# Attention on one Trainium2 core: the running sums of exponentials go from two engines to one

## The chip, the core and the metric

The kernel runs on one core of a Trainium2 chip. The core has five engines that work at the same time, each on its own queue of instructions in the order in which they were issued: TensorE (PE in the profile, with its weight loads shown apart as PEld), VectorE (DVE), ScalarE (ACT), GpSimd (POOL) and SyncE (SP), which here only issues DMA transfers. An instruction that has to wait for another engine holds up all that stands behind it on its own engine. The metric is the device time of one execution in microseconds. Lower is better.

## The reference

Three layers follow one another: attention with pooled queries, a gated feed-forward layer with RMS normalisation, and a mixture of experts with the best two of eight. The change touches the first alone, of which this is the core (batch 2, 8 heads, 1152 keys, head size 64, 576 pooled queries):

```python
q_pool = q.reshape(B, H, S // factor, factor, D).mean(axis=3)     # factor 2
scores = scale * np.matmul(q_pool, k.transpose(0, 1, 3, 2))
scores = scores - np.max(scores, axis=-1, keepdims=True)
attn = np.exp(scores)
attn = attn / (np.sum(attn, axis=-1, keepdims=True) + 1e-09)
return np.matmul(attn, v).astype(np.float32)
```

What matters below is `np.sum(attn, axis=-1)`: for each query, the sum of 1152 exponentials.

## The kernel before

Attention is worked through in 8 pairs of heads (p = 0 to 7; `NPB`), four to each batch entry. A pair has 18 steps: two halves of the queries (g, 288 each) times nine blocks of 128 keys (c). In each step `st_exp` (L198) makes the scores of 128 keys by 288 queries for both heads in PSUM (tile `st`, three buffers), and ScalarE turns them into exponentials in SBUF (tile `et`, 128 x 2 x 288, nine buffers). Keys lie on the partitions. `avmm` (L230) multiplies the exponentials by V, some steps later and in bursts (`S_AV`).

The sum over keys is made in two parts. First the nine `et` tiles of a half are added element by element into one tile of 128 partitions; then `sums` (L243) lets TensorE add up the partitions with a matmul by ones, and `sums2` (L257) brings the result to the queries' layout as `rs`. The first part is `esum` (L213), called once a step for the step before. The table `S_EP` says which engine takes a block: VectorE adds blocks 0, 2, 3, 4, 6 and 7 into `es` (five instructions, L222 for the first, L224 for the others), GpSimd adds blocks 1, 5 and 8 into `accp` (two instructions). `emerge` (L226) then adds `accp` to `es` on VectorE (L228), at the half-step that `S_EM` names. So a half costs VectorE six instructions and GpSimd two, and there are 16 halves.

The maximum that is subtracted is found from scores of their own: `s1` (L186) makes the scores of 128 queries against all 1152 keys in a PSUM tile of three banks, of which there is one buffer, and VectorE takes the maximum of each row into a column of `Ql` (L194). The next `s1` can't begin before that reduction is over. There are nine a pair. In the main loop those of pair p that are still open and the first of pair p + 1 stand at half-steps 1, 6, 10, 13, 16, 20, 21, 26 and 28 (`S_S1A`, `S_S1B`; half-steps count from 0 to 35, two to a step). `ql_trans` (L172) and `ql_trans2` (L178) transpose `Ql` on TensorE, at half-steps 29, 33 and 15; all transposes share one PSUM buffer (tag `T`), which must be read out before the next one is made.

All order is written out by hand: the code issues the instructions of every engine in the order of the loop at L439 to L513, and the tables name the half-step of each piece of work (`F[i]`). Besides the above, GpSimd splits K and Q of pair p + 2 into a rounded part and a remainder (`split`, at half-steps 20 and 24: L109 and L115 for K, L122, L109 and L124 for Q); it does this in pairs 0 to 5. In pairs 4 and 5 the finished first batch entry is transposed and scaled by `rs` (`x1`: TensorE L292, VectorE L293, then ScalarE and GpSimd L299); `x1` of tokens 1 to 4 stands in pair 5 at half-steps 10, 26, 27 and 30. In pair 6 `x2b` transposes it back (TensorE L324, ScalarE L327, VectorE L328). In pair 7 the decoding of the next layer's weights begins (VectorE L407 to L412, ScalarE L405 and L415, GpSimd L416). After attention the feed-forward layer's matmuls (L551) follow on TensorE.

Of the kernel before, what the change touches and what calls it, by code (L numbers as in the profile page):

```python
# [9 lines left out]
F32 = mybir.dt.float32  # L10
# [5 lines left out]
ALU = mybir.AluOpType  # L16
# [5 lines left out]
def fused_kernel(ctx, tc, q, k, v, w_gate, w_val, w_out, rms_g,  # L22
                 r_gate, r_noise, noise, e_w1, e_w2, out, dbg=None):
    nc = tc.nc
    P = 128
    B, H, S, D = q.shape
    NP = H // 2
    KC = S // P
# [4 lines left out]
    NG = 288  # L33
# [3 lines left out]
    pe, dve, act, pool, sp = nc.tensor, nc.vector, nc.scalar, nc.gpsimd, nc.sync  # L37
# [24 lines left out]
    NPB = B * NP  # L62
# [4 lines left out]
    ab = ax.enter_context(tc.tile_pool(name="ab", bufs=1))  # L67
# [21 lines left out]
    def load_kq(p, h):  # L89
        b, hh = p // NP, 2 * (p % NP) + h  # L90
        qr = Qraw[h]
        qv = q[b, hh].rearrange("(s t) d -> s (t d)", t=2)
        raw[p, h] = fr.tile([P, KC, D], F32, name="kraw", tag=f"kraw{h}", bufs=1)
        sp.dma_start(raw[p, h], k[b, hh].rearrange("(p c) d -> p c d", c=KC))
        sp.dma_start(qr[:, 0:4, :], qv[0:QF].rearrange("(p c) x -> p c x", c=4))
        if h == 1:
            for z in range(2):
                sp.dma_start(qr[z * QR:(z + 1) * QR, 4, :], q[b, hh - 1 + z].rearrange("(s t) d -> s (t d)", t=2)[QF:])
# [94 lines left out]
                pe.matmul(t[:, j, 0:384], QB, KJ[:, ks], start=True, stop=True)  # L193
        dve.tensor_reduce(Ql[p % 2][h][:, c, D:D + 1], t[:, :, 0:384], axis=AX.XY, op=ALU.max, negate=True)  # L194

    xT, rs, es, ET, AV, accp, smS = {}, {}, {}, {}, {}, {}, {}

    def st_exp(p, g, c, hs=(0, 1), early=False):  # L198
        if hs[0] == 0:
            ET[p, g, c] = ab.tile([P, 2, NG], F32, name="et", tag="et", bufs=9)  # L200
        et = ET[p, g, c]
        cs, n0 = slice(c * P, (c + 1) * P), g * NG
        for h in hs:
            if early:
                t = tpool[0].tile([P, 512], F32, name="st", tag="T")
                tpool.append(tpool.pop(0))
            else:
                t = ps[0].tile([P, 512], F32, name="st", tag="st", bufs=3)
            pe.matmul(t[:, 0:NG], KT[p, h][:, cs], QhT[p, h][:, n0:n0 + NG], start=True, stop=False)  # L209
            pe.matmul(t[:, 0:NG], KT2[h][p % NKT[h]][:, cs], QlT[p, h][:, n0:n0 + NG], start=False, stop=True)  # L210
            act.activation(et[:, h, :], t[:, 0:NG], AF.Exp, scale=SCALE)  # L211

    def esum(p, g, c):  # L213
        if g == 0 and c == 0:
            es[p] = ab.tile([P, 2, SQ], F32, name="es", tag="es", bufs=2)
        if c == 0:
            accp[p, g] = ab.tile([P, 2, NG], F32, name="accp", tag="accp", bufs=2)
        eg, ap, e = es[p][:, :, g * NG:(g + 1) * NG], accp[p, g], ET[p, g, c]
        z = S_EP[c]
        eng, acc, cs = (dve, eg, EPL[0]) if z == 0 else (pool, ap, EPL[1])  # L220
        if c == cs[1]:
            eng.tensor_tensor(acc, ET[p, g, cs[0]], e, op=ALU.add)  # L222
        elif c > cs[1]:
            eng.tensor_tensor(acc, acc, e, op=ALU.add)  # L224

    def emerge(p, g):  # L226
        eg = es[p][:, :, g * NG:(g + 1) * NG]
        dve.tensor_tensor(eg, eg, accp[p, g], op=ALU.add)  # L228

    def avmm(p, g, c):  # L230
        b, hp = p // NP, p % NP
        if c == 0:
            AV[p, g] = ps[0].tile([P, 512], F32, name="av", tag="av", bufs=1)
        av = AV[p, g]
        for h in range(2):
            pe.matmul(av[h * D:(h + 1) * D, 0:NG], V[p][:, h, c, :], ET[p, g, c][:, h, :],  # L236
                      start=(c == 0), stop=(c == KC - 1))
        if c == KC - 1:
            if g == 0:
                xT[p] = xp.tile([P, SQ], F32, name="xT", tag="xT", bufs=6)  # L240
            act.copy(xT[p][:, g * NG:(g + 1) * NG], av[:, 0:NG])  # L241
# [176 lines left out]
    S_S1A = (1, 6, 16, 13, 20)  # L418
    S_S1B = (10, 5, 21, 26, 28)
    S_KA = (0, 5, 2, 7)  # L420
    S_KB = (8, 18, 12, 20)
    S_QA = (14, 29)
    S_QB = (15, 33)
    S_SPA = 24
    S_SPB = 20
    S_EM = (12, 33)
    S_SUM = (17, 22)
    S_LD = (4, 34, 34)
    S_AV = (1, 5, 10, 13)
    S_X = (26, 10, 26, 27, 30, 33)  # L430
    S_X2 = (6, 22, 27, 31)
    S_EP = (0, 1, 0, 0, 0, 1, 0, 0, 1)
    S_LAG = 2
    S_W = ((1, 3, 4, 5, 8), (12, 18, 19, 20, 27), (30, 31, 32))

    S_LAST = dict(s1a=(0, 9), s1b=(12,), qa=(15,), em=(16, 28), sum=(20, 35), av=(1, 5, 7, 13, 16))
    EPL = [[c for c in range(KC) if S_EP[c] == z] for z in range(2)]
    av_q, n_av = [], 0
    for p in range(NPB):  # L439
        F = [[] for _ in range(2 * NST)]  # L440

        def at(i, f, *a):
            F[i].append((f, a))

        if p + 1 < NPB:
            at(S_LD[0], load_v, p + 1)
            for i in range(2, QC):
                at(S_S1A[i], s1, p + 1, 0, i - 2)
                at(S_S1B[i], s1, p + 1, 1, i - 2)
            for i in range(4):  # L450
                if p or i >= K_EARLY:
                    at(S_KA[i], kq_trans, p + 1, 0, i)
                at(S_KB[i], kq_trans, p + 1, 1, i)
            at(max(S_KA), kt2_copy, p + 1, 0)
            at(max(S_KB), kt2_copy, p + 1, 1)
            at(S_QA[1], ql_trans, p + 1, 0)
            at(S_QB[1], ql_trans, p + 1, 1)
        sl = S_LAST if p == NPB - 1 else dict(s1a=S_S1A, s1b=S_S1B, qa=S_QA, em=S_EM, sum=S_SUM, av=S_AV)
        at(sl["s1a"][0], s1, p, 0, 3)
        at(sl["s1b"][0], s1, p, 1, 3)  # L460
        at(sl["s1a"][1], s1, p, 1, 4)
        at(sl["qa"][0], ql_trans2, p)
        if p + 2 < NPB:
            if p == 0:
                load_kq(2, 0)
                load_kq(2, 1)
            at(S_SPA, split, p + 2, 0)
            at(S_SPB, split, p + 2, 1)
        if p == 1:
            for i in range(9):  # L470
                at(4 * i, lambda i: sp.dma_start(out[i * P:(i + 1) * P], zt), i)
        if p + 3 < NPB:
            at(S_LD[1], load_kq, p + 3, 0)
            at(S_LD[2], load_kq, p + 3, 1)
        if p:
            at(sl["em"][0], emerge, p - 1, 1)
            at(sl["sum"][0], sums, p - 1)
            at(sl["sum"][1], sums2, p - 1)
        at(sl["em"][1], emerge, p, 0)
        if p == NP:  # L480
            at(S_X[0], x1, 0, 0)
        if p == NP + 1:
            for i in range(1, QC):
                at(S_X[i], x1, 0, i)
            at(S_X[5], xr, 0)
        if p == NP + 2:
            for t, s_ in enumerate(S_X2):
                at(s_, x2, 0, t)
                at(s_ + 4, x2b, 0, t)
        if p == NPB - 1:  # L490
            fr_s.close()
            wps.append(ctx.enter_context(tc.tile_pool(name="wp", bufs=1, side="right", reuse_waits="tile")))
            at(0, w_load, 0, 0)
            at(0, w_load, 0, 1)
            for i, a in enumerate(((0, 0), (0, 1), (1, 0))):
                for k_, s_ in enumerate(S_W[i]):
                    at(s_, w_dec, *a, k_)
                if i < 2:
                    at(S_W[i][3], w_load, 1, i)
        for i in range(NST):  # L500
            g, c = divmod(i, KC)
            st_exp(p, g, c, (1,) if p == 0 and i < N_EARLY else (0, 1))
            av_q.append((p, g, c))
            for f, a in F[2 * i]:
                f(*a)
            if len(av_q) > 1:
                esum(*av_q[-2])
            if i in sl["av"]:
                while n_av < len(av_q) - S_LAG:
                    avmm(*av_q[n_av])  # L510
                    n_av += 1
            for f, a in F[2 * i + 1]:
                f(*a)  # L513
    esum(*av_q[-1])
    emerge(NPB - 1, 1)
    for a in av_q[n_av:]:
        avmm(*a)
    ax.close()
# [1129 lines left out]
```

## Time and profile before

| | |
|---|---|
| median of three runs | 777.85 us (776.69 to 778.9) |
| the profiled execution | 776.33 us |
| its span | 774.6 us |
| TensorE busy | 740.6 us (96% of the span) |
| VectorE busy | 528.6 us (68%) |
| ScalarE busy | 375.1 us (48%) |
| GpSimd busy | 256.7 us (33%) |
| granted TensorE clock, mean | 0.994 of full speed |

The profile comes from one execution. The span runs from its first instruction to its last; the device time has some 1.7 us around it. Busy time is the time in which an engine has an instruction in work; for TensorE matmuls overlap, so that a busy TensorE need not be at its peak. Attention fills the stretch from about 20 to 264 us. One pair takes about 30 us, and pair p begins near the start of its reduction at half-step 1: 21.43, 49.56, 171.70, 204.10 and 236.53 us for pairs 0, 1, 5, 6 and 7.

### The profile page before, as it was taken

What the parts mean: (1) busy time and instruction counts of PE and PEld (TensorE: products, weight loads), DVE (VectorE), ACT (ScalarE), POOL (GpSimd) and SP (SyncE); (2) the same over time, 40 slices, a digit from 0 to 9 for tenths busy, and PEclk for the clock granted to TensorE, in tenths of its full rate; (3) what the DMA queues carried; (4) which work ended last, traced back from release to release, by engine and by line L of the source; (5) the groups of instructions that cost most, each with busy time, mean ns of one, the idle gap of its engine ahead of it and who ended that gap; (6) DMA issues with size and microseconds to landing.
All of it is one profiled execution on the core that took longest, in us unless ns stands there. A gap on an engine that the chain in (4) does not pass through costs nothing. (4 is left out here: it accounts for less than half of the span.)

```text
span 774.6 us, 13461 instructions
## 1 busy us (share of the span) xinstructions
PE 740.6 (96%) x5078; PEld 613.0 (79%) x5078; DVE 528.6 (68%) x804; ACT 375.1 (48%) x766; POOL 256.7 (33%) x219
## 2 busy tenths in 40 slices
PE   6999999999999999999999999999999999999993
PEld 5777777777676669988888889987998898978761
DVE  6788778878779877657568745569756676748520
ACT  5556565656667554443142325254544455537510
POOL 8456366375713321222022310020312212432221
PEclk9999999999999999999999999999999999999997
DMA  8556243333251221332033201664998769879982
GB/s 234 146 151 186 71 124 84 93 94 91 52 150 55 67 99 55 104 113 87 23 110 109 58 1 55 218 188 153 322 358 259 212 169 278 257 239 362 351 269 46
DMA packets 74010, 118.02 MB, mean 152 GB/s; under 512 B 7383, under 2 KB 37807, under 8 KB 73936
## 3 DMA queue, kind: packets, MB, share of 16 engines
q1 hardware_dynamic: 68784, 106.27, 43.6%
q0 software_dynamic: 5152, 10.80, 6.4%
q8 instruction: 42, 0.69, 0.4%
q14 instruction: 32, 0.26, 0.1%
HBM read 98.16 MB, written 9.65 MB: 139 GB/s over the span
## 5 line engine op out<-in xcount | busy, mean ns | idle before, releaser
L551 PE MATMUL gv<-XN,ws 128*128 128x256 f32 (+2 forms) x912 | 164.8, 330 | 1.3 <-POOL ws L416 1.3
L551 PEld LDWEIGHTS gv<-XN,ws 128*128 128x128 f32 x912 | 143.3, 188 | 15.7 <-POOL ws L416 1.9
L194 DVE TENSOR_REDUCE Ql<-s 128x1 fp32r<-128x1152 f32 x72 | 97.4, 1355 | 48.7 <-PE s L191 31.9
L211 ACT ACTIVATE et<-st 128x288 f32<-128x288 f32 x288 | 103.6, 417 | 41.5 <-PE st L210 39.2
L1101 DVE TENSOR_TENSOR wz<-raw,wz 128x1024 fp32r<-128x1024 f32 x80 | 96.0, 1223 | 28.9 <-ACT wz L107 28.6
L1202 PE MATMUL py<-wz,hTT 128*128 128x512 f32 x384 | 93.8, 395 | 0.0
L209 PE MATMUL st<-QH,KT 128*128 128x288 f32 x288 | 91.5, 333 | 2.3 <-ACT et L211 1.2
L416 POOL TENSOR_TENSOR ws<-wm,ws 128x1024 fp32r<-128x1024 f32 x18 | 43.6, 2423 | 145.2 <-ACT ws L415 130.2
L572 PE MATMUL po<-ws,hT 128*128 128x512 f32 x324 | 83.2, 395 | 2.2 <-DVE X L577 2.1
L107 ACT CAST wz<-raw 128x1024 fp32r<-128x1024 f32 x80 | 81.1, 1047 | 0.4 <-PE py L1202 0.4
L210 PE MATMUL st<-QlT,KT 128*128 128x288 f32 x288 | 81.1, 295 | 0.0
L1202 PEld LDWEIGHTS py<-wz,hTT 128*128 128x128 f32 x384 | 70.0, 188 | 13.6 <-DVE hTT L1070 0.2
L236 PE MATMUL av<-et,v 128*64 128x288 f32 x576 | 77.4, 412 | 0.5 <-ACT xT L241 0.5
L209 PEld LDWEIGHTS st<-QH,KT 128*128 128x128 f32 x288 | 54.0, 187 | 22.2 <-issue 12.3
L572 PEld LDWEIGHTS po<-ws,hT 128*128 128x128 f32 x324 | 58.9, 188 | 14.2 <-DVE X L577 3.2
L224 DVE TENSOR_TENSOR es<-es,et 128x576 f32<-128x576 f32 x64 | 63.4, 991 | 1.6
L1278 POOL DMA_INDIRECT out_dram<-yo,sidx x16 | 29.3, 1832 | 96.9 <-DVE yo L1277 55.9
L236 PEld LDWEIGHTS av<-et,v 128*64 128x64 f32 x576 | 38.3, 136 | 27.8 <-issue 3.9
L1175 PEld LDWEIGHTS ph<-xgT,wz 128*128 128x128 f32 x480 | 57.7, 189 | 0.4
L1175 PE MATMUL ph<-xgT,wz 128*128 128x256 f32 x480 | 57.8, 281 | 0.0
L561 ACT CAST hT<-sl 128x256 fp32r<-128x256 f32 (+2 forms) x38 | 18.9, 497 | 74.9 <-DVE sl L560 74.9
L210 PEld LDWEIGHTS st<-QlT,KT 128*128 128x128 f32 x288 | 54.3, 189 | 0.2
(280 smaller groups left out, 1097.0 us busy)
## 6 DMA issues: line engine op xcount, KB each, us to landing
raw<-in_moe_w_dram SPq DMA_DIRECT2D x112, 512.0 KB, 9.0
wraw<-in_moe_w_gate_dram SPq DMA_DIRECT2D x6, 1024.0 KB, 6.8
wraw<-in_moe_w_val_dram SPq DMA_DIRECT2D x6, 1024.0 KB, 5.0
wraw<-in_moe_w_out_dram SPq DMA_DIRECT2D x6, 1024.0 KB, 4.8
kraw<-in_k_dram SPq DMA_DIRECT2D x16, 288.0 KB, 3.7
v<-in_v_dram SPq DMA_DIRECT2D x8, 576.0 KB, 3.7
KT<-KT SPq DMA_DIRECT2D x16, 288.0 KB, 3.1
KJ<-KT SPq DMA_DIRECT2D x16, 288.0 KB, 4.6
```

The source lines that it names most:

```text
L107: act.copy(o, i)
L194: dve.tensor_reduce(Ql[p % 2][h][:, c, D:D + 1], t[:, :, 0:384], axis=AX.XY, op=ALU.max, negate=True)
L209: pe.matmul(t[:, 0:NG], KT[p, h][:, cs], QhT[p, h][:, n0:n0 + NG], start=True, stop=False)
L210: pe.matmul(t[:, 0:NG], KT2[h][p % NKT[h]][:, cs], QlT[p, h][:, n0:n0 + NG], start=False, stop=True)
L211: act.activation(et[:, h, :], t[:, 0:NG], AF.Exp, scale=SCALE)
L224: eng.tensor_tensor(acc, acc, e, op=ALU.add)
L236: pe.matmul(av[h * D:(h + 1) * D, 0:NG], V[p][:, h, c, :], ET[p, g, c][:, h, :], start=(c == 0), stop=(c == KC - 1))
L551: pe.matmul(t[:, 0:n], w[a][:, d, j * P:(j + 1) * P], XN[hf][b_][:, d, cs], start=(k_ == 0), stop=(k_ == 11))
L572: pe.matmul(pt, HT[f, hf][a][:, j, c0:c0 + P], w[b_][:, j, :], start=(k_ == 0), stop=(k_ == 5))
L1101: eng.tensor_tensor(lo, RAW[u % 2][i], hi.bitcast(F32), op=ALU.subtract)
L1175: pe.matmul(o, w[a][:, d, j * P:j * P + P], XT[u][c][:, d], start=z + d == 0, stop=z == 2 and d == 3)
L1202: pe.matmul(PL[u, "y", k], x[c][:, f0 + d, k * P:k * P + P], w[a][:, d], start=i == 4 and z + d == 0, stop=i == 7 and z == 2 and d == 1)
```

## The change

GpSimd's share of the sums goes. `esum` adds all nine blocks of a half into `es` on VectorE: one instruction for blocks 0 and 1 together, then seven more. `accp`, `emerge` and the tables `S_EP`, `EPL` and `S_EM` are gone, and nothing else is edited.

```diff
     def esum(p, g, c):
         if g == 0 and c == 0:
             es[p] = ab.tile([P, 2, SQ], F32, name="es", tag="es", bufs=2)
-        if c == 0:
-            accp[p, g] = ab.tile([P, 2, NG], F32, name="accp", tag="accp", bufs=2)
-        eg, ap, e = es[p][:, :, g * NG:(g + 1) * NG], accp[p, g], ET[p, g, c]
-        z = S_EP[c]
-        eng, acc, cs = (dve, eg, EPL[0]) if z == 0 else (pool, ap, EPL[1])
-        if c == cs[1]:
-            eng.tensor_tensor(acc, ET[p, g, cs[0]], e, op=ALU.add)
-        elif c > cs[1]:
-            eng.tensor_tensor(acc, acc, e, op=ALU.add)
-
-    def emerge(p, g):
-        eg = es[p][:, :, g * NG:(g + 1) * NG]
-        dve.tensor_tensor(eg, eg, accp[p, g], op=ALU.add)
+        eg, e = es[p][:, :, g * NG:(g + 1) * NG], ET[p, g, c]
+        if c == 1:
+            dve.tensor_tensor(eg, ET[p, g, 0], e, op=ALU.add)
+        elif c > 1:
+            dve.tensor_tensor(eg, eg, e, op=ALU.add)
...
-    S_EM = (12, 33)
...
-    S_EP = (0, 1, 0, 0, 0, 1, 0, 0, 1)
...
-    EPL = [[c for c in range(KC) if S_EP[c] == z] for z in range(2)]
...
         if p:
-            at(sl["em"][0], emerge, p - 1, 1)
             at(sl["sum"][0], sums, p - 1)
             at(sl["sum"][1], sums2, p - 1)
-        at(sl["em"][1], emerge, p, 0)
...
     esum(*av_q[-1])
-    emerge(NPB - 1, 1)
```

Eight lines fewer stand ahead of most of the code, so that L222 becomes L218, L224 becomes L220, L293 becomes L285 and so on. How the instructions now follow one another on VectorE is shown at three places.

VectorE in pair 0, from the reduction at half-step 1 to the one at half-step 13, before (`Ql<-s` is the maximum of an `s1` tile, `es<-et` the first add of a half, `es<-es,et` a further one):

```order
L194 TENSOR_REDUCE Ql_91<-s_329 128x1
L194 TENSOR_REDUCE Ql_92<-s_356 128x1
L222 TENSOR_TENSOR es<-et 128x2x288
L224 TENSOR_TENSOR es<-es,et 128x2x288
L194 TENSOR_REDUCE Ql_92<-s_383 128x1
L224 TENSOR_TENSOR es<-es,et 128x2x288
L194 TENSOR_REDUCE Ql_93<-s_409 128x1
```

and after:

```order
L194 TENSOR_REDUCE Ql_91<-s_329 128x1
L218 TENSOR_TENSOR es<-et 128x2x288
L194 TENSOR_REDUCE Ql_92<-s_356 128x1
L220 TENSOR_TENSOR es<-es,et 128x2x288 x2
L194 TENSOR_REDUCE Ql_92<-s_383 128x1
L220 TENSOR_TENSOR es<-es,et 128x2x288 x2
L194 TENSOR_REDUCE Ql_93<-s_409 128x1
```

The first add of the half, now of blocks 0 and 1, stands ahead of the reduction at half-step 6, and two adds instead of one follow each of the next two reductions.

VectorE in pair 1, from the reduction at half-step 21 over the one at 26 to the one at 28, before (`rs` is the result of `sums2`):

```order
L194 TENSOR_REDUCE Ql_92<-s_882 128x1
L266 TENSOR_SCALAR rs_812<-xt 128x2x2 x2
L268 TENSOR_SCALAR rs_812<-xt 64x2
L222 TENSOR_TENSOR es<-et 128x2x288
L194 TENSOR_REDUCE Ql_92<-s_931 128x1
L224 TENSOR_TENSOR es<-es,et 128x2x288
L194 TENSOR_REDUCE Ql_92<-s_953 128x1
```

and after:

```order
L194 TENSOR_REDUCE Ql_92<-s_879 128x1
L258 TENSOR_SCALAR rs_810<-xt 128x2x2 x2
L260 TENSOR_SCALAR rs_810<-xt 64x2
L218 TENSOR_TENSOR es<-et 128x2x288
L220 TENSOR_TENSOR es<-es,et 128x2x288
L194 TENSOR_REDUCE Ql_92<-s_929 128x1
L220 TENSOR_TENSOR es<-es,et 128x2x288
L194 TENSOR_REDUCE Ql_92<-s_951 128x1
```

Between the reductions at half-steps 21 and 26 there are now two adds, one right behind the other, where there was one. The same holds in every pair up to pair 6.

VectorE in pair 5, from the reduction at half-step 21 to the one at 28, before (`xs<-xt,rs` is the scaling in `x1`, which frees the transposes' PSUM buffer):

```order
L194 TENSOR_REDUCE Ql_92<-s_2418 128x1
L266 TENSOR_SCALAR rs_2349<-xt 128x2x2 x2
L268 TENSOR_SCALAR rs_2349<-xt 64x2
L222 TENSOR_TENSOR es<-et 128x2x288
L194 TENSOR_REDUCE Ql_92<-s_2466 128x1
L293 TENSOR_TENSOR xs_2072<-xt,rs_812 128x512
L224 TENSOR_TENSOR es<-es,et 128x2x288
L293 TENSOR_TENSOR xs_2073<-xt,rs_812 128x512
L194 TENSOR_REDUCE Ql_92<-s_2506 128x1
```

and after:

```order
L194 TENSOR_REDUCE Ql_92<-s_2407 128x1
L258 TENSOR_SCALAR rs_2339<-xt 128x2x2 x2
L260 TENSOR_SCALAR rs_2339<-xt 64x2
L218 TENSOR_TENSOR es<-et 128x2x288
L220 TENSOR_TENSOR es<-es,et 128x2x288
L194 TENSOR_REDUCE Ql_92<-s_2456 128x1
L285 TENSOR_TENSOR xs_2064<-xt,rs_810 128x512
L220 TENSOR_TENSOR es<-es,et 128x2x288
L285 TENSOR_TENSOR xs_2065<-xt,rs_810 128x512
L194 TENSOR_REDUCE Ql_92<-s_2496 128x1
```

The added instruction is again the second add ahead of the reduction at half-step 26, and with it ahead of both scalings `xs`. On GpSimd the 32 adds into `accp` are gone, and the order of the rest is as it was; TensorE, ScalarE and SyncE issue the same instructions in the same order.

## Rows read from the trace of the kernel before

**Rows 1.** The page, part 1: busy us, share of the span, instructions

```profile
PE 740.6 (96%) x5078; PEld 613.0 (79%) x5078; DVE 528.6 (68%) x804; ACT 375.1 (48%) x766; POOL 256.7 (33%) x219
```

**Rows 2.** Busy time of one stretch: stretch, length, busy us (instructions) by engine

```profile
100.00:120.00 20.00, 19.87 (x145) 15.33 (x145) 15.67 (x16) 12.01 (x34) 10.50 (x8) 1.00 0.44 119
```

**Rows 3.** Groups by line, to 300 us: xcount | busy us, mean ns

```profile
L224 DVE TENSOR_TENSOR es<-es,et 128x576 f32<-128x576 f32 x64 | 63.4, 991 | 1.6
L228 DVE TENSOR_TENSOR es<-es,accp 128x576 f32<-128x576 f32 x16 | 18.2, 1136 | 0.3 <-issue 0.3
L222 DVE TENSOR_TENSOR es<-et 128x576 f32<-128x576 f32 x16 | 13.4, 839 | 0.0
L222 POOL TENSOR_TENSOR accp<-et 128x576 f32<-128x576 f32 x16 | 27.1, 1694 | 48.7 <-ACT et L211 48.7
L224 POOL TENSOR_TENSOR accp<-accp,et 128x576 f32<-128x576 f32 x16 | 26.0, 1625 | 33.4 <-ACT et L211 28.3 <-DVE es L224 4.7
```

**Rows 4.** Waits, 20 to 270 us: total us, times, longest us

```profile
PEld s L191 <- DVE Ql L194: 2.8, 10, 0.4
```

**Rows 5.** Timeline, pair 0, VectorE, then TensorE: start, us, instruction, [idle before]

```profile
25.80 1.88 DVE L224 TENSOR_TENSOR es<-es,et 128x576 f32<-128x576 f32 x1
27.60 1.34 DVE L194 TENSOR_REDUCE Ql<-s 128x1 fp32r<-128x1152 f32 x1
...
25.08 0.79 PE L191 MATMUL s<-KT,QH 128*128 128x384 f32 x3
29.00 0.79 PE L191 MATMUL s<-KT,QH 128*128 128x384 f32 x3 [0.28 <-DVE Ql L194]
```

**Rows 6.** Timeline, pair 1, VectorE, then GpSimd, then TensorE

```profile
69.33 1.21 DVE L222 TENSOR_TENSOR es<-et 128x576 f32<-128x576 f32 x1
71.82 1.29 DVE L224 TENSOR_TENSOR es<-es,et 128x576 f32<-128x576 f32 x1
...
69.27 0.67 POOL L109 TENSOR_SCALAR khl<-kraw 128x576 fp32r<-128x576 f32 x1
70.02 1.78 POOL L115 TENSOR_TENSOR khl<-kraw,khl 128x576 fp32r<-128x576 f32 x1
71.77 0.73 POOL L122 TENSOR_TENSOR qs<-Qraw 128x256 f32<-128x256 f32 x1
...
72.68 0.69 PE L191 MATMUL s<-KT,QH 128*128 128x384 f32 x3
```

**Rows 7.** Timeline, pair 2, VectorE, then GpSimd

```profile
99.66 0.74 DVE L222 TENSOR_TENSOR es<-et 128x576 f32<-128x576 f32 x1
...
99.61 1.32 POOL L109 TENSOR_SCALAR khl<-kraw 128x576 fp32r<-128x576 f32 x1
```

**Rows 8.** Timeline, pair 4, VectorE, then GpSimd, then TensorE

```profile
160.76 0.77 DVE L222 TENSOR_TENSOR es<-et 128x576 f32<-128x576 f32 x1
...
161.01 1.78 POOL L115 TENSOR_TENSOR khl<-kraw,khl 128x576 fp32r<-128x576 f32 x1
...
164.11 0.69 PE L191 MATMUL s<-KT,QH 128*128 128x384 f32 x3
166.28 0.37 PE L136 MATMUL tt<-identr,Ql 128*128 128x128 f32 x3
```

**Rows 9.** Timeline, pair 5, VectorE, then GpSimd, then TensorE

```profile
191.56 1.21 DVE L222 TENSOR_TENSOR es<-et 128x576 f32<-128x576 f32 x1
194.10 0.68 DVE L293 TENSOR_TENSOR xs<-xt,rs 128x512 f32<-128x512 f32 x1
...
192.25 1.79 POOL L115 TENSOR_TENSOR khl<-kraw,khl 128x576 fp32r<-128x576 f32 x1
...
194.83 0.66 PE L292 MATMUL xt<-ident,xT 128*128 128x128 f32 x4
```

**Rows 10.** Timeline, TensorE, end of pair 6 and start of the next stage

```profile
233.59 0.45 PE L136 MATMUL tt<-identr,Ql 128*128 128x128 f32 x3 [0.87 <-DVE XN L328]
270.16 0.55 PE L262 MATMUL xt<-ident,smS 128*128 128x128 f32 x3 [0.61 <-ACT smS L255]
```

More of the change, by code (lines that the diff above doesn't have):

```diff
@@ L194, in s1 @@
         dve.tensor_reduce(Ql[p % 2][h][:, c, D:D + 1], t[:, :, 0:384], axis=AX.XY, op=ALU.max, negate=True)
-    xT, rs, es, ET, AV, accp, smS = {}, {}, {}, {}, {}, {}, {}
+    xT, rs, es, ET, AV, smS = {}, {}, {}, {}, {}, {}
     def st_exp(p, g, c, hs=(0, 1), early=False):
@@ L431, in fused_kernel @@
     S_X2 = (6, 22, 27, 31)
-    S_EP = (0, 1, 0, 0, 0, 1, 0, 0, 1)
     S_LAG = 2
     S_W = ((1, 3, 4, 5, 8), (12, 18, 19, 20, 27), (30, 31, 32))
-    S_LAST = dict(s1a=(0, 9), s1b=(12,), qa=(15,), em=(16, 28), sum=(20, 35), av=(1, 5, 7, 13, 16))
-    EPL = [[c for c in range(KC) if S_EP[c] == z] for z in range(2)]
+    S_LAST = dict(s1a=(0, 9), s1b=(12,), qa=(15,), sum=(20, 35), av=(1, 5, 7, 13, 16))
     av_q, n_av = [], 0
@@ L457, in fused_kernel @@
             at(S_QB[1], ql_trans, p + 1, 1)
-        sl = S_LAST if p == NPB - 1 else dict(s1a=S_S1A, s1b=S_S1B, qa=S_QA, em=S_EM, sum=S_SUM, av=S_AV)
+        sl = S_LAST if p == NPB - 1 else dict(s1a=S_S1A, s1b=S_S1B, qa=S_QA, sum=S_SUM, av=S_AV)
         at(sl["s1a"][0], s1, p, 0, 3)
```

## The prediction

> **What bounds the kernel now.** I read the page first: TensorE is busy 96% of the span, VectorE 68%, GpSimd 33% [rows 1]. Then the busy time by stretch: in the middle of attention TensorE has 19.87 of 20 us, VectorE 15.67 and GpSimd 10.50 [rows 2]. So TensorE sets the pace, VectorE has about a fifth of its time free, and an engine's load as such decides nothing. What can cost time is a place where TensorE waits for one particular VectorE instruction. There are two kinds: the next `s1` needs the reduction of the one before it (one buffer), and a transpose needs the shared `T` buffer, which in pairs 4 to 6 a VectorE instruction frees. The waits show how tight the first kind is already: ten waits of TensorE's weight loads for a reduction, 2.8 us in all, none over 0.4 [rows 4]. Little is lost there, but little is left. I then read the timelines around each of these places.
>
> **What is removed and added.** VectorE adds into `es` 96 times before: 63.4 + 18.2 + 13.4 = 95.0 us [rows 3]. An undisturbed add takes 0.74 to 0.75 us [rows 7], so 96 would take 72; the other 23 us are VectorE standing still inside an add while GpSimd works on SBUF. The 32 adds into `accp` (27.1 + 26.0 us, rows 3) are one part of that, the splits of K and Q the other. After the change there are 16 x 8 = 128 adds, 96 us if undisturbed. VectorE is thus as busy as before, and GpSimd has 53 us less. No other engine gets or loses an instruction, no DMA is moved. What counts is which collisions go and which are new.
>
> **Pair 0, collision gone.** The add at 25.80 lasts 1.88 us with GpSimd's first `accp` add beside it, so the next reduction starts at 27.60 although its scores were ready at 25.87 (25.08 + 0.79). The following `s1` waits 0.28 us for it [rows 5]. In the new order two adds precede that reduction, which end about 26.4, and the wait goes: -0.3. What is late next is the reduction after it, behind two adds as well, but they fit into the time in which TensorE makes its scores. Bounds: 0 (another wait takes over) and -0.6 (the next `s1` gains as much again).
>
> **Half-steps 21 to 28 in pairs 1 to 5.** Here GpSimd splits K and Q, and the new order puts a second add right behind the first, ahead of the reduction at half-step 26. Pair 1 [rows 6]: GpSimd's L109 begins at 69.27 and VectorE's first add at 69.33; the add takes 1.21 instead of 0.75, so it waited until GpSimd was through, and ends at 70.54. GpSimd's next instruction, L115, asks at 70.02, stands until the add is over and ends at 71.80. The new second add would ask at 70.47, later than L115. I let the one that asked first go first, since the same timeline shows it once more: L122 from 71.77 takes its undisturbed 0.73, and the add from 71.82 takes 1.29, to 73.11, 0.61 us after L122's end. So the second add ends at 71.80 + 0.61 = 72.41, the reduction starts there and lasts 1.34 to 1.36 [rows 5], and ends about 73.70. The next `s1` follows a reduction's end by 0.06 (27.60 + 1.34 = 28.94, then 29.00, rows 5): 73.76 instead of 72.68. TensorE loses 1.1 us. In front of this `s1` nothing on TensorE can be brought forward, and all that stands behind it moves with it. Pair 3 has the same rows in the trace, with a first add of 1.21 as well: another 1.1.
>
> Pair 2 differs: VectorE's add from 99.66 takes 0.74, and GpSimd's L109 from 99.61 takes 1.32 instead of 0.67 [rows 6, 7]. Here VectorE went first. The second add then waits only for the short L109, until about 100.9, ends about 101.5, and the reduction ends about 102.9, just ahead of the `s1` that needs it (as in pair 1, 3.35 us after the first add, 103.0): 0, with bounds 0 and 1.1.
>
> At this place the Trainium skill has a rule ("SBUF — State Buffer", section "SBUF: two separate sides"): VectorE and GpSimd share a pair of ports as an exclusive lock, and whichever starts first has it for its whole instruction. Pairs 1 and 3 agree (GpSimd 0.06 us earlier, VectorE's add 1.21). Pair 2 does not: GpSimd started 0.05 us earlier and yet it was the one that waited. By the rule alone pair 2 would cost 1.1 as well, and the sum would be +6.1 instead of +5.0.
>
> Pair 4 [rows 8]: the first add runs from 160.76 to 161.53 undisturbed, L115 asks at 161.01 and ends at 162.79. The second add ends at 162.79 + 0.61 = 163.40, the reduction about 164.7, and the `s1` at 164.11 comes 0.6 late. Then its own reduction: between the two stand a scaling of 0.68 and another add, with GpSimd's last split instructions beside them. 164.7 + 0.6 + 0.7 is 166.0, the reduction ends about 167.4, and the transpose at 166.28 that reads its result comes at 167.4: +1.1. Bounds: 0 (second add not held up) and 1.7 (the third add held up in full too).
>
> Pair 5 [rows 9]: first add until 192.77, L115 until 194.04, second add until 194.65, reduction until about 195.95. Behind it stands the scaling (0.68, until 196.55), and for that the transposes at 194.83 wait: 196.6, so +1.8. Bounds: 0.5 (second add not held up: 193.45, reduction 194.75, scaling 195.35) and 2.4 (the same again at the next scaling).
>
> **Pairs 6 and 7 and the way out.** There is no split any more. In pair 6 the transposes at 233.59 already wait 0.87 us for VectorE's `XN` [rows 10], and one more add stands ahead of it: +0.75. In pair 7 VectorE is loaded with decoding, has four adds more and no merge, and loses the collisions with `accp`; I count that as even. At the start of the next stage TensorE waits 0.61 us for ScalarE's copy of the sums [rows 10], which stands behind a decode step that VectorE ends earlier once the collisions are gone, and can take that much back. Together +0.2; bounds -0.6 (only the second) and +1.5 (two adds of 0.75 late, nothing taken back).
>
> **The sum.** -0.3 + 1.1 + 0 + 1.1 + 1.1 + 1.8 + 0.2 = +5.0 us for pairs 0, 1, 2, 3, 4, 5 and the rest. The profiled execution would go from 776.33 to 781.3 us. It lies 1.5 below the median of the three runs, and it is a median that will be compared: 777.85 + 5.0 = 782.8.
>
> **Rivals.**
>
> *Two adds in a row keep the port.* If the second add goes on at once, GpSimd's L115 waits instead, which hurts nobody, since the splits are for two pairs later. Then in pair 1 the second add ends at 71.2 and the reduction at 72.5, in time for 72.68. Pairs 1, 3 and 4 cost nothing, pair 5 costs 0.5: -0.3 + 0.5 + 0.2 = +0.4, 778.2 us, no slower than can be told. It decides from the point at which VectorE's second request beats one that has waited 0.4 us. For it speaks pair 2, where the later one went first; against it, pair 1's add at 71.82, which lost by 0.05 us.
>
> *GpSimd wins everywhere, and the way out gives nothing back.* Pair 2 costs 1.1, pair 5 the 2.4, the end +1.5: -0.3 + 4 x 1.1 + 2.4 + 1.5 = +8.0, 785.9 us.
>
> *Less contention makes attention faster.* Of the 23 us in which adds stood still some part could have held TensorE up, and the time goes with them. Against it: all the waits of weight loads for reductions are 2.8 us [rows 4]. At the most these go, and the 0.6 of the way out: 777.85 - 3.4 = 774.5. The Trainium skill ("GPSIMD Engine Reference", section "Engine selection") says that elementwise work belongs on VectorE. The trace agrees as far as durations go (1625 to 1694 ns against 839 to 991, rows 3), but that rule weighs instructions, not the queue they stand in.
>
> **How the numbers follow.** A measurement of this kernel can tell some 0.3%, 2.3 us, from no change: the borders are 775.5 and 780.2. The forecast, with its own range of 780.2 to 784.5, gets 0.62, the rival of the kept port 0.22, that of GpSimd winning everywhere 0.11, the faster one 0.05. The first and third lie above 780.2, and a small part of the forecast below it: slower 0.70. The second lies between the borders: same 0.25. Faster 0.05. For eight in ten the range leaves out the faster case and the end of the slowest: 777.7 to 786.0.
>
> **What would show it.** In the profile after, at half-step 26 of pairs 1, 3, 4 and 5, an add of about 1.9 us right behind the first, and TensorE with a hole of about 1 us ahead of the next `s1` (in pair 5 ahead of `x1`'s transposes, near 1.8). In pair 2 two adds with no such hole. The wait in pair 0 is gone, and the one for `XN` in pair 6 is about 1.6. VectorE is busy about as long as before, GpSimd some 50 us less. TensorE's busy time falls in the slices of pairs 1 to 5 alone; the stages behind attention keep their lengths. If the second adds take 0.75 and GpSimd's L115 is long instead, the first rival is right. If TensorE's holes lie elsewhere, behind reductions at other half-steps or behind ScalarE, my reading of the places is wrong.

## The result, and the profile after

The kernel after takes 781.37 us (median of 7 runs, 780.3 to 781.99), the kernel before beside it 776.69 us (7 runs, 775.2 to 778.9): ratio 1.0059, 95% interval 1.0045 to 1.0073, or +4.7 us. The forecast was 782.8, with +5.0 as its sum. Timed twice more, each time beside the kernel before, the same change came to +7.0 and +5.2 us. That one kernel gives three sizes is part of the answer.

The page of the kernel after, part 1 (busy us, share, instructions), answers to [rows 1]:

```profile
PE 741.0 (95%) x5078; PEld 612.3 (79%) x5078; DVE 538.8 (69%) x836; ACT 375.3 (48%) x766; POOL 206.3 (27%) x187
```

GpSimd has lost 50.4 us and VectorE gained 10.2. TensorE's work is the same, so what was added to the span (774.6 to 778.5) is idle time of TensorE. The groups of the adds, to 300 us (xcount | busy us, mean ns), answer to [rows 3]:

```profile
L220 DVE TENSOR_TENSOR es<-es,et 128x576 f32<-128x576 f32 x112 | 94.3, 842 | 6.6 <-ACT et L211 0.5
L218 DVE TENSOR_TENSOR es<-et 128x576 f32<-128x576 f32 x16 | 13.4, 837 | 0.0
```

They are 107.7 us for 128 adds, where 96 was the undisturbed figure: 12 us of standing still are left of 23. The collisions have halved and the kernel is slower. It matters which ones are left. The waits between 20 and 275 us (total us, times, longest) answer to [rows 4]:

```profile
PEld s L191 <- DVE Ql L194: 4.1, 12, 1.1
PEld xt L284 <- DVE xs L285: 2.2, 1, 2.2
PEld tt L136 <- DVE XN L320: 1.8, 1, 1.8
```

The waits for a reduction have gone from 2.8 us, none over 0.4, to 4.1 with one of 1.1. The timeline of pair 1 after (start, us, instruction), for [rows 6]:

```profile
68.50 1.33 POOL L109 TENSOR_SCALAR khl<-kraw 128x576 fp32r<-128x576 f32 x1
68.56 0.74 DVE L218 TENSOR_TENSOR es<-et 128x576 f32<-128x576 f32 x1
...
69.40 1.04 DVE L220 TENSOR_TENSOR es<-es,et 128x576 f32<-128x576 f32 x1
69.91 1.79 POOL L115 TENSOR_TENSOR khl<-kraw,khl 128x576 fp32r<-128x576 f32 x1
...
71.91 0.69 PE L191 MATMUL s<-KT,QH 128*128 128x384 f32 x3
```

VectorE's first add got through at once and GpSimd's L109 stood. The second add waited only for L109, and the next `s1` had no hole. The same place in pair 2, for [rows 7]:

```profile
98.82 0.67 POOL L109 TENSOR_SCALAR khl<-kraw 128x576 fp32r<-128x576 f32 x1
98.88 1.21 DVE L218 TENSOR_TENSOR es<-et 128x576 f32<-128x576 f32 x1
...
99.57 1.78 POOL L115 TENSOR_TENSOR khl<-kraw,khl 128x576 fp32r<-128x576 f32 x1
100.20 1.77 DVE L220 TENSOR_TENSOR es<-es,et 128x576 f32<-128x576 f32 x1
...
101.89 1.34 DVE L194 TENSOR_REDUCE Ql<-s 128x1 fp32r<-128x1152 f32 x1
...
103.29 0.80 PE L191 MATMUL s<-KT,QH 128*128 128x384 f32 x3 [0.90 <-DVE Ql L194]
```

Here GpSimd was first. L115 asked at 99.57, ahead of the second add, and that add ended at 101.97, 0.62 us after L115. The next `s1` has a hole of 0.90 us. This is the mechanism of the prediction, step by step, but in pair 2, where it was not expected, and not in pairs 1 and 3, where it was.

In pair 4 the second add meets L115 as well, though the first add ran almost alone (0.79 us from 161.18), for [rows 8]:

```profile
161.45 1.79 POOL L115 TENSOR_TENSOR khl<-kraw,khl 128x576 fp32r<-128x576 f32 x1
162.08 1.78 DVE L220 TENSOR_TENSOR es<-es,et 128x576 f32<-128x576 f32 x1
...
168.21 0.37 PE L136 MATMUL tt<-identr,Ql 128*128 128x128 f32 x3
```

In pair 5, for [rows 9]:

```profile
194.15 1.79 POOL L115 TENSOR_TENSOR khl<-kraw,khl 128x576 fp32r<-128x576 f32 x1
...
194.78 1.78 DVE L220 TENSOR_TENSOR es<-es,et 128x576 f32<-128x576 f32 x1
...
196.48 1.34 DVE L194 TENSOR_REDUCE Ql<-s 128x1 fp32r<-128x1152 f32 x1
...
197.75 0.68 DVE L285 TENSOR_TENSOR xs<-xt,rs 128x512 f32<-128x512 f32 x1
...
198.48 0.33 PE L284 MATMUL xt<-ident,xT 128*128 128x128 f32 x1 [1.74 <-DVE xs L285]
```

The scaling `xs` stands behind add and reduction, and the transposes wait 1.74 us for it. At the end of pair 6, for [rows 10]:

```profile
235.80 1.61 DVE L220 TENSOR_TENSOR es<-es,et 128x576 f32<-128x576 f32 x2
237.33 0.69 DVE L320 TENSOR_TENSOR XN<-xt,XN 128x512 fp32r<-128x512 f32 x1
...
238.07 0.44 PE L136 MATMUL tt<-identr,Ql 128*128 128x128 f32 x3 [1.61 <-DVE XN L320]
```

Two adds stand ahead of `XN`, and the hole is 1.61 instead of 0.87.

### The profile page after: what moved, and what is told of

The parts are those of the page before. It is cut to its first block, busy times and chain, and to the rows that moved or that the text cites. A ratio compares the mean times of both kernels' runs of the same rounds, so it can differ in the third digit from the quotient of the medians.

```text
span 778.5 us, 13476 instructions
## 1 busy us (share of the span) xinstructions
PE 741.0 (95%) x5078; PEld 612.3 (79%) x5078; DVE 538.8 (69%) x836; ACT 375.3 (48%) x766; POOL 206.3 (27%) x187
## 5 line engine op out<-in xcount | busy, mean ns | idle before, releaser
L220 DVE TENSOR_TENSOR es<-es,et 128x576 f32<-128x576 f32 x112 | 94.3, 842 | 6.6 <-ACT et L211 0.5
```

Of the source, the lines that this page charges most:

```text
L220: dve.tensor_tensor(eg, eg, e, op=ALU.add)
```

## The experiments

Below, a shift is by how much the first matmul of an `s1` starts later than the same one in the first profile of the kernel before. Where it grows, time is lost.

**Splitting earlier.** In the kernel after, `S_SPA = 24` becomes `S_SPA = 16`, so that GpSimd's split at half-step 24, the later of its two, is issued before the crowded place.

> The changed kernel with GpSimd's first split of a pair moved from half-step 24 to 16, so that both splits are over when VectorE's two adds ahead of the reduction at half-step 26 begin; instructions and their number stay. Theory (the cost is the second add standing behind GpSimd's split there): the holes of pairs 2, 4 and 5 go, 1.1 + 1.5 + 1.9 = 4.5 us less than the changed kernel's 781.4, near 776.9, and no add over 1 us between half-steps 21 and 28 in any pair. Rival (the cost is VectorE's load, 32 adds more): no change, 781. Second rival (the split only collides elsewhere): 779 to 782, with holes behind the reductions at half-steps 16 or 20.

Measured: 782.43 us (781.94 to 782.7), ratio to before 1.0075 (1.0061 to 1.0088). The timeline in pair 1, where GpSimd now splits around half-step 10:

```profile
54.40 1.43 POOL L115 TENSOR_TENSOR khl<-kraw,khl 128x576 fp32r<-128x576 f32 x1
54.81 2.84 DVE L220 TENSOR_TENSOR es<-es,et 128x576 f32<-128x576 f32 x2
...
61.77 0.44 PE L191 MATMUL s<-KT,QH 128*128 128x384 f32 x1 [0.57 <-DVE Ql L194]
```

The holes at half-step 28 of pairs 1 to 4 are gone, but each of these pairs now loses about 0.28 at half-step 13 and 0.58 at half-step 16; pair 0 loses 0.1 and 0.6 there, and pair 5 still 1.3. Theory's 776.9 fell. The second rival had the mechanism, a collision elsewhere, though 782.43 lies just above its 782. At both places tried, the split meets two adds ahead of a reduction.

**Holding the adds back.** Nothing of the computation changes, only the place of the adds of steps 12 and 13 (12 to 14 in pair 5) of pairs 0 to 5: they are issued a step or two later, behind the reduction.

```diff
+    es_q, HOLD = [], {0: (12, 13), 1: (12, 13), 2: (12, 13), 3: (12, 13), 4: (12, 13), 5: (12, 13, 14)}
...
-                esum(*av_q[-2])
+                es_q.append(av_q[-2])
+            if i not in HOLD.get(p, ()):
+                while es_q:
+                    esum(*es_q.pop(0))
```

> The changed kernel, but in pairs 0 to 5 the adds of the second half's blocks 2 and 3 (in pair 5 block 4 too) are held back until the reduction at half-step 28 has been issued (in pair 5 until the last scaling too). GpSimd's splits stay where they are. Theory (what costs is the place of the second add in VectorE's queue): holes of pairs 2, 4 and 5 go, about 777.1. The burst of seven adds ahead of half-step 1 of the next pair takes 5.2 us and ends before that reduction is needed. Rival (VectorE's load): 781, since the same 128 adds are done. Second rival (any late add costs): the burst makes the reduction at half-step 1 late and TensorE waits at half-step 6; 779 or more.

Measured: 776.1 us (775.68 to 779.04), ratio 1.0000 (0.999 to 1.0011). The shift stays at -1.0 from pair 1 to pair 6. In pair 5 the transposes of `x1` start without a wait, where the kernel after had 1.74 us:

```profile
193.83 0.65 PE L284 MATMUL xt<-ident,xT 128*128 128x128 f32 x4
```

The same 128 adds are done, so the loss in pairs 1 to 5 comes from the place of the held adds (the second and third of the half, in pair 5 the fourth too), not from their number. At the end of pair 6, where no add was held, 0.75 is lost at the hole, as in the kernel after (0.74), and then 1.5 more, for which TensorE has no wait. Two stretches there (stretch, length, busy us by engine PE, PEld, DVE, ACT, POOL, then the granted clock):

```profile
232.00:236.00 4.00, 2.77 (x17) 2.57 (x18) 3.04 (x5) 3.09 (x9) 0.00 (x0) 0.86 0.00 0
236.00:238.00 2.00, 2.00 (x9) 1.63 (x9) 1.50 (x2) 1.94 (x4) 0.00 (x0) 0.50 0.03 8
```

The clock falls to its lower level, 1.2 GHz, some two microseconds after the hole of 1.61 us, and for about 3 us. In the kernel after, the same hole is followed by a clock of 1.00.

**The kernel after once more**, unchanged, to see what is chance.

> The changed kernel once more, timed beside the others and profiled anew. If who gets the SBUF first in pairs 1, 2 and 3 is decided by some hundredths of a us in each execution, another of the three pairs has the hole of 1.1 us this time, and the time stays within 781.4 +- 1. If it is fixed by the instructions, pair 2 alone has it again. Pairs 4 and 5 lose 1.5 and 1.9 either way.

Measured: 783.25 us (780.25 to 784.37), ratio 1.0096 (1.008 to 1.0111). The profiled execution, 780.25, again lost pair 2 alone; the other four took 781.5 to 784.4. The median lies outside the expected 781.4 +- 1. I first concluded from the two like profiles that the instructions fix who is first. The later runs refute that.

**Removing without replacing.** The kernel before without GpSimd's adds and without the merges:

```diff
-        eng, acc, cs = (dve, eg, EPL[0]) if z == 0 else (pool, ap, EPL[1])
+        if z:
+            return
+        eng, acc, cs = dve, eg, EPL[0]
```

> The kernel before with GpSimd's 32 adds and the 16 merges left out and nothing put in their place: blocks 1, 5 and 8 are missing from the sums, so that the output is not the reference's. It shows the first half of the change alone. Theory (GpSimd's adds collide with VectorE where nearly nothing waits for it): pair 0's 0.4 us and the 0.6 at the way out, together 0.4 to 1.2 us faster than before, near 776. Rival (contention holds attention up in general): 2 to 3.4 us faster, 773 to 775.

Its total of 1175.9 us can't be compared: its trace has 20239 instructions against 13461, for a branch that depends on the data stands behind attention. (That the missing blocks change the routing of the experts, and so the branch, is inferred.) In attention it gains 0.45 in pair 0 (the wait at 29.00) and is then flat to pair 7; at one and the same matmul of the next stage (`gv`) it is 2.1 ahead (274.23 against 276.32), of which 0.6 came in the prologue and some 1.1 on the way out of attention. Leaving out the prologue, which varies, GpSimd's adds and the merges thus cost the kernel before some 1.5 us, more than the theory's 0.4 to 1.2. The rival of contention everywhere (2 to 3.4) fell: nothing is gained between pair 0 and pair 7, though with the prologue counted the 2.1 would reach its range.

**The kernel before once more.**

> The kernel before, unchanged, for a second profile of it. Two theories on the 0.6 us by which its first profile was later than all four profiles without GpSimd's sum already ahead of pair 0. (a) Chance of one execution: in this profile the first scores of pair 0 come as early as in the kernel after, within 0.1 us. (b) Something in the instructions: again 0.6 us later. On who goes first between GpSimd's L109 and VectorE's first add at half-step 24: if it is fixed by the instructions, the first adds of pairs 1, 3 and 5 last 1.2 us again and that of pair 2 0.74; if it is chance, the pairs are mixed otherwise.

777.82 us in one execution. In pair 1:

```profile
69.16 1.33 POOL L109 TENSOR_SCALAR khl<-kraw 128x576 fp32r<-128x576 f32 x1
69.21 0.74 DVE L222 TENSOR_TENSOR es<-et 128x576 f32<-128x576 f32 x1
```

In [rows 6] the same two instructions took 0.67 and 1.21. So the one kernel has it both ways: who is first changes from execution to execution. The prologue came 0.2 earlier than in the first profile, against 0.3 to 0.7 in the other kernels; it varies too, and I take nothing from it. This execution is 1.5 us longer than the first, all of it in one stretch of 512 to 516 us where the clock is at the lower level.

**Pair 6 held as well.** As the held kernel, with `6: (15,)` added to `HOLD`.

> The kernel with the adds held in pairs 0 to 5 (776.1 us), and in pair 6 the add of step 15 held as well, so that as many adds as in the kernel before stand ahead of XN there. Theory: the hole of TensorE ahead of the transposes near 233 us goes from 1.61 back to 0.87, TensorE's granted clock does not fall to half behind it, and of the 2.2 us that the held kernel lost between pair 6 and the middle of pair 7 nearly all goes; the way out, which gave 1.1 of them back, gives less: 774.3 to 775.4. Rival 1: the clock falls without that hole, then 775.4 to 775.8 and the low clock is seen again in pair 7. Rival 2: the end of pair 7 is set by something else (VectorE's decoding), then 776.1 unchanged.

775.44 us (774.6 to 776.77, 12 runs), ratio 0.9982 (0.9971 to 0.9993): faster than both kernels, if only by 0.9 us. The timeline:

```profile
231.14 0.75 DVE L220 TENSOR_TENSOR es<-es,et 128x576 f32<-128x576 f32 x1
231.92 0.69 DVE L320 TENSOR_TENSOR XN<-xt,XN 128x512 fp32r<-128x512 f32 x1
...
232.67 0.45 PE L136 MATMUL tt<-identr,Ql 128*128 128x128 f32 x3 [0.87 <-DVE XN L320]
```

One add, a hole of 0.87 as before, no fall of the clock, and a shift of -0.9 to the middle of pair 7: so far the theory held. Behind that 0.4 is lost in pair 7, which the kernel with pairs 0 to 5 held did not lose there, and the median lies just above the expected 774.3 to 775.4.

**Pair 5 alone held.** The kernel after, with `HOLD = {5: (12, 13, 14)}`.

> The kernel after, with the adds of pair 5's steps 12 to 14 held to step 15, and nothing else changed. Theory: pair 5's term of 1.9 us goes and the others stay (pair 2 1.1, pair 4 about 0.6 to 1.5, pair 6 0.75): 1.9 less than the kernel after, 779.5. Rival: a hole filled in pair 5 opens behind it, since the adds are only moved into the next pair: 781 or more. If TensorE's clock falls behind the hole in pair 6 as with all pairs held, up to 1.2 of the gain is lost: 780.7.

781.22 us (778.52 to 782.36). In the profiled execution (778.52, the shortest) pair 5 loses nothing (in the kernel after 1.72 and 0.2), and nothing opens behind it; the clock falls behind the hole of pair 6 (1.0 more than in the kernel after by the next stage). But pair 2 also lost nothing, though no instruction before it had changed:

```profile
98.97 1.34 POOL L109 TENSOR_SCALAR khl<-kraw 128x576 fp32r<-128x576 f32 x1
99.03 0.74 DVE L218 TENSOR_TENSOR es<-et 128x576 f32<-128x576 f32 x1
...
99.88 1.03 DVE L220 TENSOR_TENSOR es<-es,et 128x576 f32<-128x576 f32 x1
```

So the term of pair 5 is shown in the trace. The expected 779.5 was missed: in the medians a change of 1.9 us can't be told here from the variation of the other pairs. The rival's 781 or more fits the median, but the hole behind pair 5 that it needs is not in the trace.

**Both adds of pair 6 held**, `6: (14, 15)`.

> As the last but one, with the adds of both steps 14 and 15 of pair 6 held, so that no add at all stands between the reduction and XN. Theory: the hole near 233 us shrinks from 0.87 to 0.1 or 0.2, below that of the kernel before, and the time is another 0.7 lower than with one add held: 773.6 to 774.7, faster than both kernels. Rival: the three adds in a row at the start of pair 7 hold back the reduction that its first scores need by up to 1.5 us: 775 to 776, with the hole there.

775.76 us (775.03 to 779.09), ratio 0.9994 (0.9982 to 1.0006). Theory fell: without any add ahead of it, `XN` waits for ScalarE, and TensorE's hole stays. The rival's 775 to 776 came true, and there is a hole of 0.57 us for a VectorE reduction in pair 7 (at 245.32), later in the pair than it said.

```profile
231.73 0.69 DVE L320 TENSOR_TENSOR XN<-xt,XN 128x512 fp32r<-128x512 f32 x1 [0.70 <-ACT XN L319]
...
232.48 0.45 PE L136 MATMUL tt<-identr,Ql 128*128 128x128 f32 x3 [0.86 <-DVE XN L320]
```

**Deciding who is first.** To settle what the pairs cost, I moved one engine by some hundredths of a microsecond. In the first kernel GpSimd executes one small memset ahead of L109, in the second VectorE one ahead of its first add, each in pairs 1 to 3 of the kernel after; the third is the kernel after itself.

```diff
+            if 1 <= p <= 3:
+                at(S_SPA, pool.memset, late, 0.0)
             at(S_SPA, split, p + 2, 0)
```

```diff
+            if i == 11 and 1 <= p <= 3:
+                dve.memset(late, 0.0)
             if len(av_q) > 1:
                 esum(*av_q[-2])
```

> The kernel after, with one small memset of GpSimd (128x16, its value is used by nothing) ahead of its L109 at half-step 24 of pairs 1, 2 and 3, so that L109 asks a little later. In the profiles so far VectorE's first add there took 0.74 where it began at most 0.06 us after L109, and 1.2 where it began 0.06 or 0.07 after it; the same kernel had it both ways. Theory (who is first by some hundredths of a microsecond decides 1.1 us per pair, anew in each execution): all three first adds take 0.74 to 0.75, no hole ahead of the next scores in pairs 1 to 3, the profiled execution 1.1 below that of the kernel after: 779.2, and the median of the timed ones 779 to 780, with less spread. Rival (the three pairs do not decide the timed runs, which vary by TensorE's clock): no difference to the kernel after that exceeds 0.5 us.

> The kernel after, with one small memset of VectorE (128x16, its value is used by nothing) ahead of its first add at the same place of pairs 1, 2 and 3, so that GpSimd's L109 always asks first. Theory: all three first adds take 1.2, the second adds about 1.8, and TensorE has a hole ahead of the next scores in each of the three pairs, 1.1 us each: 3.2 more than with GpSimd late, 782.4 to 783, with less spread than the kernel after. By the prediction's rule for pairs 1 and 3, taken for all three, this is the case of GpSimd winning everywhere in them. Rival: as above, no difference over 0.5 us.

> The kernel after, unchanged, beside the two: by the theory its executions lie between them, each with one, two or three of the pairs lost: median 780.5 to 783.3, spread 3 us or more. The profiled execution shows one of these cases, not always pair 2 alone. By the rival it is the same as both.

Measured on one chip, before 775.77 us: GpSimd late 779.88 (779.64 to 782.98; ratio 1.0056, 1.0039 to 1.0072), VectorE late 784.32 (783.52 to 784.74; 1.0102, 1.0089 to 1.0115), the kernel after 781.01 (779.1 to 783.97; 1.0069, 1.0048 to 1.009). Pair 2 with GpSimd late:

```profile
99.23 0.11 POOL L495 MEMSET late<- 128x16 f32 x1
...
99.31 1.29 POOL L109 TENSOR_SCALAR khl<-kraw 128x576 fp32r<-128x576 f32 x1
99.33 0.74 DVE L218 TENSOR_TENSOR es<-et 128x576 f32<-128x576 f32 x1
```

Pair 3 with VectorE late:

```profile
131.75 0.67 POOL L109 TENSOR_SCALAR khl<-kraw 128x576 fp32r<-128x576 f32 x1
131.84 1.19 DVE L218 TENSOR_TENSOR es<-et 128x576 f32<-128x576 f32 x1
...
133.13 1.78 DVE L220 TENSOR_TENSOR es<-es,et 128x576 f32<-128x576 f32 x1
...
136.22 0.80 PE L191 MATMUL s<-KT,QH 128*128 128x384 f32 x3 [0.89 <-DVE Ql L194]
```

Pair 1 of the kernel after, this time (in its first profile 0.74, above):

```profile
68.79 0.67 POOL L109 TENSOR_SCALAR khl<-kraw 128x576 fp32r<-128x576 f32 x1
68.85 1.22 DVE L218 TENSOR_TENSOR es<-et 128x576 f32<-128x576 f32 x1
```

With GpSimd late the shift is flat through pairs 1 to 3, with VectorE late each of them loses 1.06 and another 0.12 just behind, 3.5 in all. The kernel after lost pairs 1 and 2 this time, and its runs spread over most of what lies between the two others. In the rows the theory held: all six first adds went as it said. In the medians the two tipped kernels are clearly apart, so the rival fell; GpSimd late and the kernel after are not (their intervals overlap). The expected 782.4 to 783 was missed: the medians differ by 4.4 where 3.2 was expected and 3.5 stand in the traces; the rest is open, since timed runs leave no rows. Both profiled executions had the fall of the clock near the end of pair 6, worth about 1.0 us, and four of the six runs with GpSimd late lie 0.9 to 1.3 us below its profiled one (780.9), so that a different share of such falls would do; that is argued, not shown.

## Why the prediction was right, and where it was not

The forecast, +5.0, came near +4.7, and the mechanism is shown, but that the sum came so near is partly luck. By the rows, the profiled execution loses about 4.6 us from pair 0 to the next stage, after a start 0.7 us earlier than in the first profile of the kernel before; that start varies from execution to execution. As for the mechanism: holding the adds back takes the loss of pairs 1 to 5 away, and tipping the order at one instruction adds or removes 1.2 us per pair. By its own steps:

- **Pair 0, -0.3.** The wait at [rows 5] went, and 0.44 was gained at half-step 13. The bound "another wait takes over" came true: 0.36 is lost at half-step 28 of the same pair and 0.11 behind it, where the second add is late by GpSimd's split too (a hole of 0.19 at 41.46). Together about -0.1.
- **Pairs 1 and 3, +1.1 each, pair 2 0.** The size is right (1.06 and 0.12 behind it, where the pair is lost), and so is the working: second add 0.62 after L115's end, where 0.61 was taken. What failed is the step that read from one execution who goes first, as if it belonged to the pair. In the first profile after, pairs 1 and 3 lost nothing and pair 2 lost; two losses were forecast, one came, by another pair. The sum came out near because the two errors partly cancel: which pair lost was luck.
- **Pair 4, +1.1.** The first part, 0.6, is 0.65. The second came to 0.86: the add between the reductions took 0.92, and the reduction at 166.51 was followed by scores that waited 0.21 and 0.15 us for ScalarE before the transposes' turn. Together 1.5, inside the bound of 1.7.
- **Pair 5, +1.8.** 1.72, and 0.2 behind it.
- **Pairs 6 and 7 and the way out, +0.2.** The hole for `XN` grew by 0.74, as worked out, and the wait of 0.61 us at the way out is gone. Pair 7, counted as even, lost 0.4, and the way out gave back 1.0, more than the 0.6 allowed for it; together +0.1. What was missing: behind that larger hole the clock can fall. Where it did, 1.5 us were lost behind the hole, but not the 0.4 in pair 7, so that 1.0 to 1.1 remained.
- **VectorE's busy time.** It was to stay about as before, with 96 us for the adds. It rose by 10.2 us, and the adds took 107.7: the collisions with the splits were priced for TensorE, but not counted here.

Of the rivals, that two adds in a row keep the port is refuted: where GpSimd was first, and in pair 4, L115 went ahead of the second add each time, and where VectorE was first, the waiting L109 did. The one of GpSimd winning everywhere is no rival but one end of the same distribution: made certain in pairs 1 to 3, it gives 784.32, +8.5 on the kernel before, where that rival had said +8.0 (from partly other terms: pair 5 stayed at 1.9). That less contention is faster has a true core of 0.9 us, which appears only when the adds are held.

The rule of the Trainium skill that was weighed ("SBUF — State Buffer", section "SBUF: two separate sides"), that whichever starts first has the ports for its whole instruction, holds for the second half, each loser standing until the other is through. By the recorded starts it holds only roughly for the first half: in 18 such meetings of the six profiles of before, after and the kernel with pair 5 held, GpSimd always started first, by 0.04 to 0.07 us, and VectorE still went ahead 11 times, with 0.04 to 0.06 us of delay; GpSimd went ahead 7 times, with 0.06 or 0.07. Even this delay does not decide alone: in pair 5 of the second profile of the kernel after, GpSimd went ahead with 0.05. Whether a recorded start is the moment at which an engine asks for the memory, no run here shows.

## What to carry to other kernels

What one engine does to another through memory depends on the instruction that stands behind in the queue: put work that nobody waits for behind the instruction that TensorE needs next, not ahead of it. When a profile shows two instructions that ask within a tenth of a microsecond of each other, who won there is one draw: work out both outcomes, and expect the time to spread between them. Holding adds until the reduction, or `XN`, is out turned a change that was 0.6% slower into one that is 0.2% faster, with the same instructions.

## What the runs showed of the hardware that was not expected

- The order of VectorE and GpSimd at the same memory can be tipped by some hundredths of a microsecond, and one kernel's executions differ in it: three memsets of 0.07 us on VectorE moved a kernel's median from 781.0 to 784.3 us.
- Behind a hole of TensorE of 1.6 to 1.7 us at the end of pair 6 its granted clock fell to half for about 3 us in five profiles of eight; behind one of 0.86 or 0.87 at the same place in none of five. In two other profiles (the kernel before, again, and the one with blocks left out) it fell near 512 us, where the longest hole just ahead was 0.60 and 0.71 us. What decides it stays open.
